# Where the column pass and the low-rank join stand in a fused 2-D DFT and mixer kernel

## The chip, the core and the metric

The kernel runs on one core of a Trainium2 chip. The core has a matrix engine (TensorE, PE in the profile), a vector engine (VectorE, DVE), an activation engine (ScalarE, ACT), a general engine (GpSimd, POOL) and a queue engine that issues transfers (SyncE, SP). Each engine works through its own queue in order and waits on semaphores for the others. Transfers run on 16 shared DMA engines; here GpSimd and SyncE issue nearly all of them. The metric is device time in microseconds for one execution; lower is better.

## The reference

Eight batches of 3136 rows by 256 channels. The first half takes the real part of a two-dimensional Fourier transform, the second half a mixer with a low-rank product over the rows and a two-layer product over the channels:

```
X = fft(x, axis=1); X = fft(X, axis=2); y = X.real          # per batch, 3136 x 256
h = (y^T @ U) @ V                                           # U 3136x32, V 32x3136
u = y + h^T
out = u + relu(u @ w_ch1) @ w_ch2                           # 256 -> 1024 -> 256
```

## The kernel before, in words

**Transform.** The real part needs cosine times cosine minus sine times sine. The symmetries of both are used: rows and channels are first added to and subtracted from their mirror images, so that products run over a quarter of the data. `fold(b)` does this on VectorE (lines 386, 395, 399) from the tiles xf (rows forward) and xr (rows backward), which `load_half` fills for the batch after it by four GpSimd-issued transfers per half (lines 55, 86, 101, 103). `seq` (line 485) multiplies with the sine and cosine tables over the rows and leaves tiles A and B; beside them it leaves the product with U in 32 further columns (tile tf, line 492). `chan` (batches 0 and 1) or `even_ch` and `odd_ch` (later batches) then transform over the channels (lines 631, 633, 643, 652) and give tiles S and T, the two mirror halves of y.

**The first channel.** Channel 0 has no mirror image and is left out of the wide products. For batches 0 and 1, `first_channel` runs a narrow product over it (`narrow`, line 556: sixteen products with 32 columns of weights), evicts it on ScalarE (lines 560, 563) into tiles evc and evo, and adds and subtracts the two parts (lines 570, 573, 574); the result is row 32 of tile va, and two copies (line 622) mirror it. For batches 2 to 7 (six together) this is the column pass: `column_loads` issues 28 transfers of single elements on SyncE into cf and cr (lines 530, 539); `column_steps` has seven steps: two casts on ScalarE (line 590), one small fold product (lines 596, 599) with its eviction (line 601) and two VectorE sums (line 603), the narrow product, two steps of sums on GpSimd into tiles tc, rows and tcb (lines 570 to 574), and a last step that mirrors rows (line 610) and copies tcb to trow (line 611, a transfer on SyncE).

**The low-rank part.** `joined(b)` adds the two halves of tf into tile tab (line 468, on GpSimd); for batches 2 and up it also copies that batch's piece of trow into tab (line 672, GpSimd) and its row of rows into row 32 of va (line 673, a transfer on SyncE). `lowrank(b)` multiplies tab with the channel tables (line 678) and ScalarE evicts the product into ta (line 680). There are two va and two ta tiles, used in turn by even and odd batches. `last_row` fills one more row of va on VectorE (line 684).

**The mixer.** The 8 x 3136 rows are taken in 49 chunks of 512. `front(c)` multiplies ta and va for a chunk (line 709) and VectorE adds S and T to it, giving u (line 725); `turned` transposes u by a SyncE transfer (line 703). `first_product` (line 735) multiplies u with w_ch1 into one of three buffers p, and ScalarE applies the relu (line 737). `second_product` (line 751) multiplies with w_ch2 one chunk later; VectorE adds the transposed u (lines 757, 759, 760) into tile o, of which there are three, and SyncE stores a chunk (line 765).

**What sets the order.** The main loop has eight slots a chunk (`8 * c + j`); in each slot stand a step of the first product, every second slot one of the second, and whatever steps of the next batch's transform a table `due` holds for that slot. `front(c + 1)` follows slot `8 * c + 3`. `spread` lays a list of steps evenly over a range of slots; batch 1's 23 transform steps lie over slots 23 to 42, and batch 2's transform ends at slot 90. From chunk 1 on, a planner reorders each engine's queue from the given order by its own estimates, except for instructions that `pin` keeps in program order, so a step that moves in the table can move its neighbours in every queue.

Of the kernel before, what the change touches and what calls it, by code (L numbers as in the profile page):

```python
# [27 lines left out]
def kernel(  # L28
# [261 lines left out]
    def kp(i):  # L290
        return KP if i == NI - 1 else PQ
# [174 lines left out]
    def join_t(eng):  # L466

        eng.tensor_tensor(TS, TF[:, :, 0], TF[:, :, 1], op=AL.add)  # L468
# [76 lines left out]
    def narrow(nb, stationary, dst, tc_, total, tag=("dft", 3), late=None, eng=None):  # L545

        t = {}
        eng = eng or nc.vector

        def products():  # L550
            pt = t["pt"] = psum.tile([P, QW], FP32, tag=tag[0], name="ptc", bufs=tag[1])
            for n in range(NI // 2):
                for g in range(4):
                    pn, par = divmod(g, 2)
                    i = ktiles(pn)[n]
                    nc.tensor.matmul(pt[g * R:(g + 1) * R], stationary(par, i),
                                     tabs[1][:kp(i), i, par, :],
                                     start=(n == 0), stop=(n == NI // 2 - 1))
            t["ev"] = wp.tile([P, QW], FP32, tag="ev", name="evc", bufs=4)
            nc.scalar.copy(t["ev"][2 * R:], t["pt"][:2 * R])  # L560
            if eng is nc.gpsimd:
                t["pt"] = wp.tile([P, QW], FP32, tag="ev", name="evo", bufs=4)
                nc.scalar.copy(t["pt"][2 * R:], pt[2 * R:])
        yield products

        def sums(par):
            e, o = (t[k][(2 + par) * R:(2 + par) * R + nb] for k in ("ev", "pt"))
            up = dst[:, HALF // 2 - par:(0 if par else None):-2]
            dn = dst[:, HALF // 2 + 2 - par:HALF + 1 - par:2]
            eng.tensor_tensor(tc_[:, par], o[:, NQ:QW], e[:, NQ:QW], op=AL.add)  # L570
            if par and total is not None:
                eng.tensor_tensor(total, tc_[:, 0], tc_[:, 1], op=AL.add)
            eng.tensor_tensor(up, o[:, par:NQ], e[:, par:NQ], op=AL.add)
            down = lambda: eng.tensor_tensor(dn, e[:, 1:NQ], o[:, 1:NQ], op=AL.subtract)  # L574
            if late is None:
                down()
            else:
                late.append(down)
        for par in range(2):
            yield lambda par=par: sums(par)  # L580

    def column_steps():
        ec = cpool.tile([KP, 2, NI, NB], BF16, name="ec")
        tc_ = cpool.tile([NB, 2, R], FP32, name="tc")

        cb = [cpool.tile([KP, 2, NI, NB], BF16, name=f"cb{t}", tag=f"cb{t}") for t in range(2)]

        def lower(t):
            with tc.issue_after(LAST[0].ins):
                nc.scalar.copy(cb[t][:], (cf, cr)[t][:])  # L590
        for n in range(2):
            yield lambda n=n: lower(n)

        def fold_c():
            pc = psum.tile([KP, 2, NI, NB], FP32, tag="dft", name="pc", bufs=3)
            nc.tensor.matmul(pc.rearrange("p a i b -> p (a i) b"), flip[:KP, 0, :KP],
                             cb[0].rearrange("p a i b -> p (a i) b"), start=True, stop=False)
            for a in range(2):
                nc.tensor.matmul(pc[:, a], flip[:KP, 1, :KP], cb[1][:, a, ::-1],
                                 start=False, stop=(a == 1))  # L600
            nc.scalar.copy(ec[:], pc[:])
            for par in range(2):
                nc.vector.tensor_tensor(GC[par][:, :NI * NB].rearrange("p (i b) -> p i b", b=NB), ec[:, 0], ec[:, 1],
                                        op=AL.add if par == 0 else AL.subtract)
        yield fold_c
        yield from narrow(NB, lambda par, i: GC[par][:kp(i), i * NB:i * NB + R], rows, tc_,
                          tcb[:], eng=nc.gpsimd)

        def finish():
            nc.gpsimd.tensor_copy(rows[:, HALF + 1:S], rows[:, HALF - 1:0:-1])  # L610
            nc.sync.dma_start(out=trow.rearrange("o (b r) -> o b r", b=NB), in_=tcb[:])
        yield finish

    def first_channel(b, **kw):
        dst = VA[b][R:R + 1]
        yield from narrow(1, lambda par, i: G[b][par][:kp(i), i, 256:256 + R], dst, TF[:1, 0],
                          None, **kw)
        mid = (HALF + S) // 2
        for lo, hi in ((HALF + 1, mid), (mid, S)):
            def turn_row(lo=lo, hi=hi):  # L620
                if b:
                    nc.gpsimd.tensor_copy(dst[:, lo:hi], dst[:, S - lo:S - hi:-1])  # L622
                    return
                with tc.issue_after(LAST[0].ins):
                    nc.scalar.copy(dst[:, lo:hi], dst[:, S - lo:S - hi:-1])
            yield turn_row

    def chan(b, lo, hi, h, tag=("dft", 3), dve=False):
        d = ST[b]
        pt = psum.tile([P, CH], FP32, tag=tag[0], name="pst", bufs=tag[1])  # L630
        nc.tensor.matmul(pt[:, :hi - lo], MC[:, h * P:(h + 1) * P], d["A"][:, lo:hi],
                         start=True, stop=False)
        nc.tensor.matmul(pt[:, :hi - lo], MSN[:, h * P:(h + 1) * P], d["B"][:, lo:hi],
                         start=False, stop=True)
        (nc.vector.tensor_copy if dve else nc.scalar.copy)(
            d["ST"[h]][:, lo:hi], pt[:, :hi - lo])
# [31 lines left out]
    def joined(b):  # L668

        join_t(nc.gpsimd)  # L670
        if b >= B0:
            nc.gpsimd.tensor_copy(TS[:1, 0], trow[:, (b - B0) * R:(b - B0 + 1) * R])
            nc.sync.dma_start(out=VA[b % 2][R:R + 1, :], in_=rows[b - B0:b - B0 + 1, :])

    def lowrank(b, tag=("dft", 3)):
        pt = psum.tile([P, 256], FP32, tag=tag[0], name="ptt", bufs=tag[1])
        for typ in range(2):
            nc.tensor.matmul(pt[:], TAB[:, typ * R:typ * R + P], MDT[typ][:], start=(typ == 0),
                             stop=(typ == 1))
        nc.scalar.copy(TA[b % 2][:R, :], pt[:R])  # L680

    def last_row(b):
        d = ST[b]
        nc.vector.tensor_tensor(VA[b % 2][2 * R:2 * R + 1, HALF + 1:S], d["S"][0:1, HALF - 1:0:-1],
                                d["T"][0:1, HALF - 1:0:-1], op=AL.subtract)
# [84 lines left out]
    def transform(b):  # L770

        for par in range(2):
            for typ in (1, 0):
                for pn in range(2):
                    yield lambda par=par, typ=typ, pn=pn: seq(b, par, typ, pn)
        if b < B0:
            row = list(first_channel(b, eng=nc.gpsimd))
            yield from row[:3]
            for ch in range(4):
                for h in range(2):  # L780
                    yield lambda ch=ch, h=h: chan(b, ch * 392 + (1 if ch else 0),
                                                  (ch + 1) * 392 + 1, h)
            yield from row[3:]
            yield lambda: (joined(b), last_row(b))
            yield lambda: lowrank(b)
            return
        for ch in range(4):
            yield lambda ch=ch: (even_ch(b, ch), across(b, ch, False))
            yield lambda ch=ch: (odd_ch(b, ch), across(b, ch, True), ch < 3 or joined(b))
        yield lambda: lowrank(b)  # L790
# [193 lines left out]
    for step in piece(1, 0) + piece(1, 1, tag=("p2", 2)) + late[2:] + late[:2]:  # L984
# [8 lines left out]
    due = {2: piece(2, 0), 3: piece(2, 1), 8: piece(3, 0),  # L993
           9: piece(3, 1), 10: piece(0, 0), 11: piece(0, 1), 13: [lambda: last_row(0)],
           16: narrow_0[3:4], 18: narrow_0[4:5]}
# [6 lines left out]
    for b in range(1, B):  # L1002
        hi = 8 * (b * S // CH - 1) + 2
        if b == 1:
            spread(list(fold(b)), 4, 23)
            spread(list(transform(b)), 23, hi)
        else:
            spread(list(fold(b)), hi - 66, hi - 35)
            spread(list(transform(b)), hi - 33, hi)
        if b == B0:  # L1010
            for at, step in zip((19, 18, 16, 15, 14, 13, 6), column_steps()):
                due.setdefault(hi - at, []).append(step)
    for n, step in enumerate(column_loads()):
        due.setdefault(8 + 15 * n // 7, []).append(step)
    for c in range(NCH + 1):
        if c == 1:
            order.close()
# [41 lines left out]
```

## Time and profile before

| | us |
|---|---|
| median of 3 runs | 448.58 |
| lowest and highest run | 448.21, 449.38 |
| the profiled execution's own time | 448.78 |
| its span in the profile | 446.7 |
| TensorE matmul busy | 435.9 |
| VectorE busy | 354.0 |
| ScalarE busy | 297.1 |
| GpSimd busy | 83.6 |

The profile is of one execution. Times within it count from the start of the span. Of each instruction it gives the start, the duration, the engine, the line of the kernel, the tiles written and read (buffer numbers left out) and their shape; a line with x8 stands for eight instructions in a row. Matmuls are pipelined and their ends are modelled, so the distance of two starts says more than a duration. In brackets stands how long the engine was idle ahead of the instruction and what ended that. The granted TensorE clock is full in all slices.

### The profile page before, as it was taken

What the parts mean: (1) busy time and instruction counts of PE and PEld (TensorE: products, weight loads), DVE (VectorE), ACT (ScalarE), POOL (GpSimd) and SP (SyncE); (2) the same over time, 40 slices, a digit from 0 to 9 for tenths busy, and PEclk for the clock granted to TensorE, in tenths of its full rate; (3) what the DMA queues carried; (4) which work ended last, traced back from release to release, by engine and by line L of the source; (5) the groups of instructions that cost most, each with busy time, mean ns of one, the idle gap of its engine ahead of it and who ended that gap; (6) DMA issues with size and microseconds to landing.
All of it is one profiled execution on the core that took longest, in us unless ns stands there. A gap on an engine that the chain in (4) does not pass through costs nothing.

```text
span 446.7 us, 8094 instructions
## 1 busy us (share of the span) xinstructions
PE 435.9 (98%) x2959; PEld 316.5 (71%) x3012; DVE 354.0 (79%) x838; ACT 297.1 (67%) x564; POOL 83.6 (19%) x144
## 2 busy tenths in 40 slices
PE   8999999999989999999999999999999999999997
PEld 6547666777666777777777777777777777777775
DVE  8979998788997789978998789978998776443433
ACT  8867647555975569756785569655885669656562
POOL 8973219200371002300211002300000000000000
PEclk9999999999999999999999999999999999999999
DMA  7997987985579337683599537792333333434343
GB/s 141 216 238 189 222 163 145 208 148 94 145 184 225 95 105 209 192 188 73 149 209 201 111 119 207 189 182 70 95 117 93 80 114 73 114 100 117 96 123 113
DMA packets 103249, 65.36 MB, mean 146 GB/s; under 512 B 73806, under 2 KB 99624, under 8 KB 100464
## 3 DMA queue, kind: packets, MB, share of 16 engines
q1 hardware_dynamic: 97528, 39.10, 40.1%
q0 software_dynamic: 5664, 25.75, 21.7%
q8 instruction: 23, 0.38, 0.4%
q14 instruction: 16, 0.13, 0.1%
q10 hardware_dynamic: 18, 0.00, 0.0%
HBM read 29.33 MB, written 25.69 MB: 123 GB/s over the span
## 4 chain that ended last, share of the span: by engine, by line
PE 76%; POOL 8%; DMA 6%; DVE 6%; issue 3%; DVEq 0%; POOLq 0%
PE p L751 34%; PE p L735 30%; DMA xf<-in_x_dram,xidx 5%; PE ph L709 4%; PE pt L485 4%; PE ptq L446 2%; DMA va<-rows 1%; DVE eof L386 1%; DVE eor L386 1%; PE pst L643 1%; PE pst L652 1%; DVE u L725 1%; POOL va L574 1%; POOL va L622 1%; POOL rows L574 1%
## 5 line engine op out<-in xcount | busy, mean ns | idle before, releaser
L737 ACT ACTIVATE h<-p 128x512 bf16<-128x512 f32 x392 | 221.8, 597 | 123.0 <-PE p L735 103.8
L735 PE MATMUL p<-u,w 128*128 128x512 bf16 x734 | 209.9, 379 | 1.3 <-DVE B L504 0.2
L751 PE MATMUL p<-w,h 128*128 128x256 bf16 x1568 | 203.7, 273 | 1.2
L751 PEld LDWEIGHTS <-h 128*128 128x128 bf16 x1568 | 153.2, 98 | 51.0 <-issue 0.3
L735 PEld LDWEIGHTS <-w 128*128 128x128 bf16 x784 | 106.0, 144 | 33.8 <-issue 0.5
L757 DVE TENSOR_TENSOR o<-p,ut 128x4 f32<-128x4 f32 (+1 forms) x100 | 16.2, 162 | 57.1 <-PE p L751 54.7
L760 DVE TENSOR_TENSOR o<-p,ut 128x254 f32<-128x254 f32 (+1 forms) x100 | 40.7, 407 | 0.0
L759 DVE TENSOR_TENSOR o<-p,ut 128x254 f32<-128x254 f32 (+1 forms) x100 | 40.7, 407 | 0.0
L468 POOL TENSOR_TENSOR tab<-tf 128x64 bf16<-128x64 f32 x7 | 3.1, 442 | 180.7 <-DVE tf L492 180.6
L386 DVE TENSOR_TENSOR eor<-xr 99x1024 bf16<-99x1024 f32 x28 | 34.5, 1236 | 0.1
L725 DVE TENSOR_TENSOR u<-ph,T 128x512 bf16<-128x512 f32 (+23 forms) x63 | 34.3, 555 | 0.2 <-PE ph L709 0.2
L386 DVE TENSOR_TENSOR eof<-xf 99x1024 bf16<-99x1024 f32 x28 | 34.4, 1244 | 0.0
L725 DVE TENSOR_TENSOR u<-ph,S 128x512 bf16<-128x512 f32 (+23 forms) x63 | 34.4, 555 | 0.0
L709 PE MATMUL ph<-va,ta 128*128 128x512 bf16 (+15 forms) x124 | 28.6, 328 | 1.6 <-DMA va<-rows 1.5
L55 POOL DMA_INDIRECT xf<-in_x_dram,xidx x14 | 17.1, 1220 | 61.9 <-DVE eof L386 50.5
L485 PEld LDWEIGHTS <-g 98*128 98x128 bf16 (+1 forms) x152 | 14.7, 98 | 13.2 <-issue 0.7
L395 DVE TENSOR_TENSOR eos<-eof,eor 99x1024 bf16<-99x1024 bf16 (+1 forms) x28 | 20.5, 748 | 0.0
L654 DVE TENSOR_TENSOR S<-evd,pst 128x392 bf16<-128x392 f32 (+1 forms) x24 | 13.5, 563 | 7.2 <-PE pst L652 4.9
L485 PE MATMUL pt<-tabs,g 98*128 98x425 bf16 x80 | 17.6, 344 | 0.0
L457 DVE TENSOR_TENSOR ev<-ptq,ex 128x131 f32<-128x131 f32 (+1 forms) x24 | 6.9, 289 | 12.7 <-ACT ex L450 12.7
L399 DVE TENSOR_TENSOR g<-eos 99x2048 bf16<-99x2048 bf16 (+1 forms) x14 | 17.0, 1218 | 0.0
L485 PE MATMUL pt<-tabc,g 98*128 98x425 bf16 x72 | 15.5, 344 | 0.0
(198 smaller groups left out, 380.2 us busy)
## 6 DMA issues: line engine op xcount, KB each, us to landing
out_dram<-o SPq DMA_DIRECT2D x48, 512.0 KB
xr<-in_x_dram POOLq DMA_DIRECT2D x14, 784.0 KB, 8.2
xb<-in_x_dram POOLq DMA_DIRECT2D x2, 392.0 KB, 6.8
ut<-u SPq DMA_TRANSPOSE x49
w<-in_moe_w_ch_dram POOLq DMA_DIRECT2D x1, 512.0 KB
out_dram<-o SPq DMA_DIRECT2D x4, 128.0 KB
va<-in_moe_V_dram POOLq DMA_DIRECT2D x2, 196.0 KB
w<-in_moe_w_ch_dram POOLq DMA_DIRECT2D x1, 256.0 KB, 6.1
```

The lines of the kernel that those rows point to most:

```text
L55: nc.gpsimd.indirect_dma_start(out_, None, bass.AP(t.tensor, t.offset, [[w, rows], [1, w]]), bass.IndirectOffsetOnAxis(idx, 0), element_of ...
L386: pin(nc.vector.tensor_tensor(dst[:, a, :, part * P:(part + 1) * P].rearrange("p i (k t) -> p i k t", k=2), lo, hi, op=AL.subtract if part ...
L395: pin(nc.vector.tensor_tensor(EOS[:, a, :, cols], EOF_[:, a, :, cols], EOR_[:, a, ::-1][:, :, cols], op=op))
L399: pin(nc.vector.tensor_tensor(G[b % 2][par][:, :, cols], EOS[:, 0, :, cols], EOS[:, 1, :, cols], op=AL.add if par == 0 else AL.subtract))
L485: nc.tensor.matmul(pt[:], g[:kp(i), i, P * typ:P * (typ + 1)], tabs[typ][:kp(i), i, par, :], start=(n == 0), stop=(n == NI // 2 - 1))
L709: nc.tensor.matmul(ph, TA[b % 2][:k, s * P:(s + 1) * P], VA[b % 2][:k, lo:hi], start=start, stop=True)
L725: nc.vector.tensor_tensor(u[:, s, col:col + hi - lo], ph[:, col:col + hi - lo], src, op=AL.add)
L735: nc.tensor.matmul(p1[:], W1[:, s, j::JT], k["u"][:, s, :], start=(s == 0), stop=(s == 1))
L737: LAST[0] = nc.scalar.activation(k["h"][:, j, :], p1[:], AF.Relu)
L751: nc.tensor.matmul(p2[:, t % w, :], h[:, j, rs], W2[:, j, :], start=(j == 0), stop=(j == JT - 1))
L759: nc.vector.tensor_tensor(o[:, ts, 1:P], p2[:, :w, 1:P], ut[:, ts, 1:P], op=AL.add)
L760: nc.vector.tensor_tensor(o[:, ts, P + 1:D], p2[:, :w, P + 1:D], ut[:, tT, P - 1:0:-1], op=AL.add)
```

## The change

Three edits, and no instruction is added or taken away.

- In batch 1's list of transform steps, `joined(1)` (line 468) is put into the same step as the second narrow sum; it stood behind the eight channel steps and the two mirroring copies, together with `last_row`. `last_row` now stands in one step with `lowrank`, so the list has 22 steps over the same slots instead of 23.
- The seven steps of the column pass stand 24, 23, 21, 20, 19, 18 and 12 slots ahead of slot 90 instead of 19, 18, 16, 15, 14, 13 and 6: slots 66, 67, 69, 70, 71, 72 and 78 instead of 71, 72, 74, 75, 76, 77 and 84.
- The 28 column loads stand two slots apart (slots 8 to 62) instead of 15/7 of a slot (8 to 65).

```
         if b < B0:
             row = list(first_channel(b, eng=nc.gpsimd))
-            yield from row[:3]
+            yield from row[:2]
+            yield lambda: (row[2](), joined(b))
             for ch in range(4):
                 for h in range(2):
                     yield lambda ch=ch, h=h: chan(b, ch * 392 + (1 if ch else 0),
                                                   (ch + 1) * 392 + 1, h)
             yield from row[3:]
-            yield lambda: (joined(b), last_row(b))
-            yield lambda: lowrank(b)
+            yield lambda: (lowrank(b), last_row(b))
             return
...
         if b == B0:
-            for at, step in zip((19, 18, 16, 15, 14, 13, 6), column_steps()):
+            for at, step in zip((24, 23, 21, 20, 19, 18, 12), column_steps()):
                 due.setdefault(hi - at, []).append(step)
     for n, step in enumerate(column_loads()):
-        due.setdefault(8 + 15 * n // 7, []).append(step)
+        due.setdefault(8 + 2 * n, []).append(step)
```

In the built program the queues differ as follows around these steps. GpSimd: the join of batch 1 stands directly behind its six narrow sums; the sums of the column pass, the mirror copy (line 610) and the first copy of line 672 stand ahead of the loads xf and xr that stood before and among them. SyncE: the copy to trow (line 611) stands one transpose and one output store sooner, and the first copy of line 673 directly behind the output store that follows it, two transposes sooner than before. TensorE: the column pass's small product stands ahead of the last group of batch 2's row products, and its sixteen narrow products directly behind that group.

More of the change, by code (lines that the diff above doesn't have):

```diff
@@ L777, in transform @@
             row = list(first_channel(b, eng=nc.gpsimd))
-            yield from row[:3]
+            yield from row[:2]
+            yield lambda: (row[2](), joined(b))
             for ch in range(4):
@@ L783, in transform @@
             yield from row[3:]
-            yield lambda: (joined(b), last_row(b))
-            yield lambda: lowrank(b)
+            yield lambda: (lowrank(b), last_row(b))
             return
@@ L1010 @@
         if b == B0:
-            for at, step in zip((19, 18, 16, 15, 14, 13, 6), column_steps()):
+            for at, step in zip((24, 23, 21, 20, 19, 18, 12), column_steps()):
                 due.setdefault(hi - at, []).append(step)
     for n, step in enumerate(column_loads()):
-        due.setdefault(8 + 15 * n // 7, []).append(step)
+        due.setdefault(8 + 2 * n, []).append(step)
     for c in range(NCH + 1):
```

## The prediction

> **What bounds the kernel now.** I read the page first, then the list of waits for TensorE's own, then TensorE's timeline at each of them, then the queues that feed those places.
>
> ```profile
> span 446.7 us, 8094 instructions
> PE 435.9 (98%) x2959; PEld 316.5 (71%) x3012; DVE 354.0 (79%) x838; ACT 297.1 (67%) x564; POOL 83.6 (19%) x144
> PE 76%; POOL 8%; DMA 6%; DVE 6%; issue 3%; DVEq 0%; POOLq 0%
> ```
>
> TensorE is busy for 98% of the span, so time is won only where TensorE itself stands still. The chain nevertheless gives 8% to GpSimd and 6% to DMA: stretches in which TensorE's next product was held by them. The list of waits has three such places, all at L678, the low-rank product that needs tile tab, and at L709, the product that needs the column row in va. A listed wait counts from the last modelled end; what it costs is better read from the starts in TensorE's timeline (start, duration, line, tiles, count, and in brackets the idle time before and what ended it):
>
> ```profile
> 76.55 1.04 PE L751 MATMUL p<-w,h 128*128 128x256 bf16 x8
> 78.09 0.28 PE L678 MATMUL ptt<-msn,tab 128*128 128x256 bf16 x1 [0.51 <-POOL tab L468]
> ...
> 128.02 0.81 PE L735 MATMUL p<-u,w 128*128 128x512 bf16 x3
> 129.36 0.28 PE L678 MATMUL ptt<-msn,tab 128*128 128x256 bf16 x1 [0.54 <-POOL tab L672]
> ...
> 132.53 0.82 PE L735 MATMUL p<-u,w 128*128 128x512 bf16 x3
> 134.88 0.48 PE L709 MATMUL ph<-va,ta 128*128 128x384 bf16 x2 [1.53 <-DMA va<-rows]
> ```
>
> The chain gives the undisturbed pace:
>
> ```profile
> 78.48 0.86 PE p L735 x4
> 79.35 0.87 PE p L751 x8
> ```
>
> So eight L751 take 0.87 us, and three L735 take 0.65. Without a wait the three products would have begun at 76.55 + 0.87 = 77.42, at 128.67 and at 133.18. The waits cost 0.67, 0.69 and 1.70 us: **3.06 us together**, and that is what the change aims at.
>
> **Part 1: the join of batch 1 directly behind its narrow sums.** No work is added or removed. GpSimd's queue now:
>
> ```profile
> 71.64 1.47 POOL L574 TENSOR_TENSOR va<-evc,evo 1x392 bf16<-1x392 f32 x1
> 73.05 0.60 POOL L86 DMA_DIRECT2D xr<-in_x_dram  x1
> 74.21 2.56 POOL L622 COPY va<-va 1x783 bf16<-1x783 bf16 x2
> 76.86 1.18 POOL L468 TENSOR_TENSOR tab<-tf 128x64 bf16<-128x64 f32 x1
> ```
>
> The join L468 moves ahead of the issue of the load xr and its edge (1.1 us to 74.21) and of two copies (2.56). It starts at about 73.1 and ends by 74.3 even with its 1.18, and TensorE wants it at 77.42: 3 us of cover. **-0.67 us.** What comes late next is the two copies, now ending by about 78.0 instead of 76.77:
>
> ```profile
> 66.51 0.38 PE L735 MATMUL p<-u,w 128*128 128x512 bf16 x1 [0.21 <-DVE B L504]
> 80.06 0.60 PE L709 MATMUL ph<-va,ta 65*128 65x64 bf16 x4
> ```
>
> The products that read va of batch 1 follow at 80.06 less 0.67, so 1.4 us remain. The load xr is issued 1.2 us later at most, and belongs to the next batch's fold. One step less in batch 1's list also makes the planner lay the last two transform products directly ahead of the narrow products. It reorders the same products; the 0.21 us wait on VectorE (first row) can go, and a wait of its size twice over can come, since ScalarE has more evictions in a row there. I bound it at -0.2 to +0.5 us and take 0, because no instruction is added.
>
> **Part 2: the column pass five slots sooner.** In the changed program's queues the sixteen column products (L556) follow the last ordinary product of batch 2 instead of starting at 114.90. Rows of today's place:
>
> ```profile
> 108.31 0.89 PE L485 MATMUL pt<-tabs,g 98*128 98x425 bf16 x4
> 114.90 1.00 PE L556 MATMUL ptc<-tabc,gc 98*32 98x425 bf16 x16
> 117.14 0.33 PE L643 MATMUL pst<-A,me 128*128 128x392 bf16 x1 [0.16 <-ACT evo L563]
> ...
> 113.95 1.01 POOL L55 DMA_INDIRECT xf<-in_x_dram,xidx  x1 [4.05 <-DVE eof L386]
> 120.21 0.24 POOL L570 TENSOR_TENSOR tc<-evo,evc 6x32 f32<-6x32 f32 x1 [4.67 <-DMA xf<-in_x_dram,xidx]
> 125.51 0.60 POOL L86 DMA_DIRECT2D xr<-in_x_dram  x1
> 126.68 1.48 POOL L610 COPY rows<-rows 6x1567 bf16<-6x1567 bf16 x1
> ```
>
> The products go to about 109.2 (the four pt end issuing 0.72 after 108.31; the small fold product pc adds 0.2). Their eviction ended 2.2 us behind their start (117.1, where the last TensorE row waited for it), hence now at 111.4. Today the sums wait 3.1 us more, until 120.21, because the load xf is ahead of them on GpSimd; in the new order it stands behind the sums and that wait goes. From sums to the end of the mirror copy is 128.16 - 120.21 = 7.95 us, less 1.12 for the two xr issues (125.56 to 126.68) that also move behind: 6.8, ending at about 118.2 instead of 128.16. So tab's corner (L672) is ready some 8 us before 128.67: **-0.69 us**.
>
> The load xf itself comes some 5 to 8 us later than 113.95, and xr behind it somewhat sooner than 125.51; the folds that read them begin only here, so I cost that at nothing:
>
> ```profile
> 165.36 2.35 DVE L386 TENSOR_TENSOR eof<-xf 99x1024 bf16<-99x1024 f32 x2
> ```
>
> The row copy into va is on SyncE:
>
> ```profile
> 111.39 0.38 SPq L765 DMA_DIRECT2D out_dram<-o  x1
> 118.03 1.23 SPq L703 DMA_TRANSPOSE ut<-u  x1
> 124.50 0.77 SPq L611 DMA_DIRECT2D trow<-tcb  x1
> ...
> 128.79 6.05 DMA va<-rows
> ```
>
> On SyncE's queue L611 now stands directly ahead of the store of 111.39, and the row copy L673 between that store and the transpose of 118.03. L673 is issued when the mirror is done, 118.3 to 121; what it holds up is that transpose, by at most 3 us. Even with today's 6.05 us (last row, from the chain) it lands by 127.3; its product is due at 133.18 - 0.67 - 0.69 = 131.8, or 0.7 sooner since its products are now ahead of three L735. **-1.70 us.** The 0.3 us before 117.14, where a product waited for the column eviction, should also go, since that product now comes 1.7 us behind the evictions: **-0.3**.
>
> The 28 loads keep their number and their SyncE queue (0.86 us each below); 3 slots fewer in all. The last pair now follows the transpose of 99.13:
>
> ```profile
> 99.13 1.26 SPq L703 DMA_TRANSPOSE ut<-u  x1
> 102.34 1.72 SPq L539 DMA_DIRECT2D cr<-in_x_dram  x2
> ...
> 104.70 0.60 ACT L737 ACTIVATE h<-p 128x512 bf16<-128x512 f32 x1 [0.56 <-PE p L735]
> ```
>
> The last is issued at about 101.3; ScalarE's cast of cr now stands behind the activation of 104.70, at 105.3. No row shows this load landing. Nearest on the same queue: trow, issued 124.50 and used at 128.16, at most 3.7 us; the upper end is va's 6.05. So 105.0 (no wait) to 107.4, which would hold ScalarE and the activations queued behind the cast for 2 us; TensorE has three p buffers to fill meanwhile, so about 1 us would reach it. I take 0, by trow, which is the nearer in size.
>
> Against the change stands VectorE. The moved sums now meet its folds:
>
> ```profile
> L386 DVE TENSOR_TENSOR eof<-xf x28: 1207/1216/2008, 37.2 to 332.2; 99x1024 bf16<-99x1024 f32 x28
> 127.23 2.01 DVE L386 TENSOR_TENSOR eof<-xf 99x1024 bf16<-99x1024 f32 x1
> 111.28 2.35 DVE L386 TENSOR_TENSOR eof<-xf 99x1024 bf16<-99x1024 f32 x2
> 117.32 0.68 DVE L725 TENSOR_TENSOR u<-ph,S 128x512 bf16<-128x512 f32 x1
> 123.98 0.17 DVE L757 TENSOR_TENSOR o<-p,ut 128x4 f32<-128x4 f32 x1 [0.20 <-PE p L751]
> 126.03 0.68 DVE L725 TENSOR_TENSOR u<-ph,T 128x512 bf16<-128x512 f32 x1
> 119.97 0.59 PE L735 MATMUL p<-u,w 128*128 128x512 bf16 x2
> ```
>
> The fold at 127.23 ran beside the mirror copy of 126.68 and took 0.8 us over its median. The two folds of 111.28 and the one that follows them will now run beside the sums. The add ahead of them comes about 1 us later, because its product is now behind the column products (1.00). VectorE's u, done at 118.0, is read at 119.97: 1.97 us of cover. So u is late by between 1.0 - 1.97, nothing, and 1.0 + 3 x 0.8 - 1.97 = 1.4 us. I take 0.6, near the middle, as the folds need not all meet a long sum: **+0.6**. In return the fold of 127.23 is free of the mirror copy, which VectorE needs when TensorE arrives early near 131.
>
> [...]
>
> **Sum.** -0.67 - 0.69 - 1.70 - 0.3 + 0.6 = -2.8 us. The profiled execution took 448.78 us (span 446.7 and 2.1 around it), 0.2 above the median 448.58 of the runs. 448.78 - 2.8 = 446.0, so the median should come to **445.8**.
>
> **Rivals.** A change of 0.3% is 1.35 us here, about what a measurement can tell from none.
>
> First: nothing is given back. If the folds slip between the sums, u is in time: -3.4, or -3.6 with the gain of the reshuffle: **445.1**. For it: 1.97 us of cover; against it: the 2.01 row.
>
> Second: VectorE becomes the bound. u late by 1.4 and the reshuffle's 0.5: -2.8 + 0.8 + 0.5 = -1.5: **447.1**. For it: VectorE is 79% busy over the span, and today's 0.8 us stretch is a fact.
>
> Third: the row is late all the same, so the change doesn't do its main part: the row goes behind an output store and beside the 784 KB loads xf and xr, now issued together. It would have to take over 10 us; then the last 1.70 stays and the gain is 1.1: **447.5**. Against it: today's 6.05 stands behind a transpose and beside such a load. [...]
>
> ```profile
> xr<-in_x_dram POOLq DMA_DIRECT2D x14, 784.0 KB, 8.2
> ```
>
> Fourth, slower: SyncE is parked. L611 and L673 now stand ahead of the output store of 111.39 and of the transpose of 118.03. If the sums end no sooner than today (trow issued at 124.50), that store is issued at 125.3 and lands 5.4 us later (estimate: 512/784 of xr's time to landing), at 130.7; the add of 123.98, three output buffers on, waits 6.7 us for it, and u behind it (126.03) ends at 134.0, where TensorE wants it at 128.02. 6.0 us lost, less the 3.06: **451.5**. It decides once trow's source comes after about 124; I have it 4.3 us behind the sums' start, at 116 to 118.
>
> **How the numbers follow.** Forecast 0.62, first rival 0.10, second 0.15, third 0.07, fourth 0.06. The page quoted first, the waits and the order agree on where the time goes, so the forecast has most. Range 444.7 to 447.1: it leaves out the third and fourth and edges of the others. Faster by over 0.3% (below 447.23): forecast, first rival and most of the second, 0.86; same 0.08; slower 0.06. The forecast's own range is 445.3 to 446.4.
>
> **What would show it.** Right: no TensorE wait at L678 for tab L468 or L672 and none at L709 for rows; L570 of the column straight behind evo near 111; L386 folds over 1.6 us near 112 to 118; a wait of about 0.6 us of L735 on VectorE's u near 119. Wrong: a ScalarE wait at L590 on the loads, or a wait for rows that is left near 131, or SyncE's store held past 118.

## The result and the profile after

The changed kernel takes **447.2 us** (median of 7 runs, 446.29 to 447.51) against 448.58 (median of 7, 448.21 to 449.58). The ratio is 0.9962, with a 95% interval of 0.995 to 0.9974: faster by 1.4 us, where 2.8 were forecast, and 0.1 us above the forecast's range. The profiled execution took 447.31 us with a span of 445.2, against 448.78 and 446.7.

The page of the changed kernel (span, busy times, and the chain by engine):

```profile
span 445.2 us, 8087 instructions
PE 435.7 (98%) x2960; PEld 316.4 (71%) x3012; DVE 353.1 (79%) x838; ACT 297.5 (67%) x564; POOL 85.7 (19%) x144
PE 91%; DVE 2%; DMA 2%; issue 1%; POOL 1%; ACT 1%; DVEq 0%; POOLq 0%
```

TensorE's share of the chain rose from 76 to 91%; GpSimd's 8% and DMA's 6% are nearly gone. TensorE's waits in the changed kernel (engine, operation, what it waited for; total, times, longest), without a first one of 1.4 us at the program's start (1.3 before) and three of 0.2 us:

```profile
PE m L850 <- DMA xb<-in_x_dram,xidx: 0.5, 2, 0.3
PE pst L643 <- DVE T L654: 0.4, 1, 0.4
PE m L850 <- DMA xb<-in_x_dram: 0.3, 1, 0.3
```

All three stalls are gone from L678 and L709. A wait of L643 for VectorE's T is new. The waits of L850 for the loads xb lie in the first 16 us, which the change doesn't touch. TensorE's timeline at these places, after:

```profile
31.17 1.52 PE L735 MATMUL p<-u,w 128*128 128x512 bf16 x6
...
71.99 0.38 PE L735 MATMUL p<-u,w 128*128 128x512 bf16 x1
72.52 0.38 PE L709 MATMUL ph<-va,ta 65*128 65x512 bf16 x1
...
77.86 1.04 PE L751 MATMUL p<-w,h 128*128 128x256 bf16 x8
78.73 0.27 PE L678 MATMUL ptt<-msn,tab 128*128 128x256 bf16 x1
...
117.30 0.33 PE L643 MATMUL pst<-A,me 128*128 128x392 bf16 x1 [0.36 <-DVE T L654]
...
120.67 0.82 PE L735 MATMUL p<-u,w 128*128 128x512 bf16 x2
...
131.77 1.04 PE L751 MATMUL p<-w,h 128*128 128x256 bf16 x8
132.64 0.61 PE L709 MATMUL ph<-va,ta 65*128 65x128 bf16 x4
```

L678 follows its eight L751 by their 0.87 us, and the four L709 stand together at 132.64 with no wait for the row. Three gaps are new, read from start to start: 0.31 us at 72.52 (one L735 takes 0.22), 0.52 at 117.30, and 0.23 within the two L735 of 120.67 (0.82 long where 0.60 is usual). The first L735 starts at 31.17; in the profile of before it was 30.17. So part of what the stalls gave up seems to have gone into the first 31 us. The experiments had to say whether that belongs to the change.

### The profile page after: what moved, and what is told of

Same layout as the page of the kernel before. It is cut to its first block, busy times and chain, and to the rows that moved or that the text cites. A ratio compares the mean times of both kernels' runs of the same rounds, so it can differ in the third digit from the quotient of the medians.

```text
span 445.2 us, 8087 instructions
## 1 busy us (share of the span) xinstructions
PE 435.7 (98%) x2960; PEld 316.4 (71%) x3012; DVE 353.1 (79%) x838; ACT 297.5 (67%) x564; POOL 85.7 (19%) x144
## 4 chain that ended last, share of the span: by engine, by line
PE 91%; DVE 2%; DMA 2%; issue 1%; POOL 1%; ACT 1%; DVEq 0%; POOLq 0%
PE p L751 38%; PE p L735 35%; PE pt L485 6%; PE ph L709 5%; DMA xb<-in_x_dram,xidx 2%; PE ptq L446 2%; PE pst L643 1%; PE pst L652 1%; PE m L850 1%; PE ptc L556 1%; ACT h L737 0%; DVE eor L386 0%; PE pst L631 0%; DVE eof L386 0%; PE pst L633 0%
## 5 line engine op out<-in xcount | busy, mean ns | idle before, releaser
L735 PE MATMUL p<-u,w 128*128 128x512 bf16 x735 | 209.3, 379 | 1.2 <-DVE B L500 0.2
L751 PE MATMUL p<-w,h 128*128 128x256 bf16 x1568 | 203.0, 273 | 1.4
L751 PEld LDWEIGHTS <-h 128*128 128x128 bf16 x1568 | 153.2, 98 | 50.4 <-DVE o L760 0.3
L735 PEld LDWEIGHTS <-w 128*128 128x128 bf16 x784 | 106.1, 144 | 35.1 <-issue 2.0
L468 POOL TENSOR_TENSOR tab<-tf 128x64 bf16<-128x64 f32 x7 | 3.1, 440 | 179.2 <-DVE tf L492 179.1
L386 DVE TENSOR_TENSOR eof<-xf 99x1024 bf16<-99x1024 f32 x28 | 35.8, 1293 | 0.0
L709 PE MATMUL ph<-va,ta 128*128 128x512 bf16 (+15 forms) x124 | 28.6, 328 | 0.3
L395 DVE TENSOR_TENSOR eos<-eof,eor 99x1024 bf16<-99x1024 bf16 (+1 forms) x28 | 19.2, 702 | 0.0
```

Of the source, the lines that this page charges most:

```text
L386: pin(nc.vector.tensor_tensor(dst[:, a, :, part * P:(part + 1) * P].rearrange("p i (k t) -> p i k t", k=2), lo, hi, op=AL.subtract if part ...
L395: pin(nc.vector.tensor_tensor(EOS[:, a, :, cols], EOF_[:, a, :, cols], EOR_[:, a, ::-1][:, :, cols], op=op))
L709: nc.tensor.matmul(ph, TA[b % 2][:k, s * P:(s + 1) * P], VA[b % 2][:k, lo:hi], start=start, stop=True)
L735: nc.tensor.matmul(p1[:], W1[:, s, j::JT], k["u"][:, s, :], start=(s == 0), stop=(s == 1))
L751: nc.tensor.matmul(p2[:, t % w, :], h[:, j, rs], W2[:, j, :], start=(j == 0), stop=(j == JT - 1))
```

## The experiments

### How much of it is the start, and how large were the stalls

Both kernels were run once more without an edit.

> The kernel before, unchanged, once more, for the scatter of the first 31 us. Theory (the start varies from execution to execution with the landing of the first loads of x): median within 0.3 us of the kernel before, single times spread over 1 us or more, and the first L735 begins at 30.2 or up to 1 us later. Rival (the start belongs to the program): the first L735 at 30.2 us as before, and single times within 0.5 us.

> The changed kernel unchanged, once more, beside the others. Theory: the three stalls stay gone whatever the start, so its time follows its start: first L735 near 30.2 us would give a span of 444.2, near 31.2 us one of 445.2; median 447.2 within 0.4 us. Rival: the stalls come back in part in another execution; a gap at L678 or L709 near 78, 129 or 133 us, and a median of 448 us.

The kernel before: 449.12 us (12 runs, 447.9 to 452.78), ratio to the other runs of before 1.0012 (0.9992 to 1.0031). The changed kernel: 447.15 us (9 runs), ratio 0.9971 (0.9962 to 0.9981), first L735 at 31.29, span 445.3, none of the three stalls. The profiled execution of the repeated kernel before (TensorE's timeline, and from the chain the row's transfer with its duration):

```profile
31.02 1.52 PE L735 MATMUL p<-u,w 128*128 128x512 bf16 x6
...
78.91 0.28 PE L678 MATMUL ptt<-msn,tab 128*128 128x256 bf16 x1 [0.48 <-POOL tab L468]
...
128.82 0.81 PE L735 MATMUL p<-u,w 128*128 128x512 bf16 x3
130.12 0.28 PE L678 MATMUL ptt<-msn,tab 128*128 128x256 bf16 x1 [0.49 <-POOL tab L672]
...
133.29 0.82 PE L735 MATMUL p<-u,w 128*128 128x512 bf16 x3
134.80 0.49 PE L709 MATMUL ph<-va,ta 128*128 128x384 bf16 x2 [0.69 <-DMA va<-rows]
```
```profile
129.57 5.18 DMA va<-rows
```

The same program started its first L735 0.85 us later than in the first profile, and yet its span is 446.7 again. The row landed at 134.75, where it had landed at 134.84: its transfer took 5.18 us where it took 6.05. So the stall at L709 was 134.80 - 133.29 - 0.65 = 0.86 us, not 1.70, while those at L678 stayed at 0.65. **The late start was swallowed by the stall for the row.** The three stalls together were 2.2 us here. With part 1 alone the row landed at 134.64, after 5.43 us, with the first L735 at 31.05. In 13 profiled executions of the kernels told of here the first L735 started between 30.16 and 31.29, in eight of them after 31.0; the first profile of before was one of the early ones, and its row transfer the slowest of the four in which the column pass stands in its old place. The start belongs to the execution and not to the program, and it goes with the landing of the first loads of x: the last two of them (xb) are issued at 5.75 and 6.64 us in the first profile of before and at 5.74 and 6.64 in that of the changed kernel, while xb's loads take 6.8 to 8.1 us from issue to landing in the one and 7.9 to 9.1 in the other. Where TensorE has no wait for xb its first L735 starts at 30.16 or 30.17 (three profiles), where it waits for 0.3 to 1.1 us in all, at 30.56 to 31.29 (the other ten). Why these loads land sooner or later, and why the row lands at nearly the same time whatever the start, stays open.

### One part at a time

Three kernels. The first has only the edit of batch 1's list:

```diff
-            yield from row[:3]
+            yield from row[:2]
+            yield lambda: (row[2](), joined(b))
...
-            yield lambda: (joined(b), last_row(b))
-            yield lambda: lowrank(b)
+            yield lambda: (lowrank(b), last_row(b))
```

The second has only the two edits of the column pass, the third only the upper one of them, with the loads at their old spacing:

```diff
-            for at, step in zip((19, 18, 16, 15, 14, 13, 6), column_steps()):
+            for at, step in zip((24, 23, 21, 20, 19, 18, 12), column_steps()):
...
-        due.setdefault(8 + 15 * n // 7, []).append(step)
+        due.setdefault(8 + 2 * n, []).append(step)
```

> Part 1 alone (the join of batch 1 directly behind its narrow sums). Forecast's term: the wait of L678 for tab near 78 us goes, -0.67 us, and nothing comes in its place: 447.9 us. Rival read from the trace of the changed kernel: the two transform products laid side by side cost 0.3 us near 72 us, so that only 0.36 us is left: 448.2 us. Both expect no TensorE wait for tab L468 of batch 1, and the waits of 0.69 and 1.70 us near 129 and 135 us unchanged. If the changed program as such starts 1 us later (its first L735 at 31.17 us and not at 30.17 us), this one shows it or not: by the theory that it is chance from run to run, the medians hide it.

> Part 2 alone (column pass five slots sooner, loads two slots apart). Forecast's terms: -0.69 -1.70 -0.3 +0.6 = -2.1 us: 446.5 us. By the trace of the changed kernel the loss to VectorE is about 0.7 us, which gives the same within 0.1. Rival: the row's place was worth less than the waits show, because the work behind is held by VectorE instead: -1.0 us, 447.6 us. All expect no wait at L678 for L672 and none at L709 for rows.

> Column steps five slots sooner, but the loads at their old spacing, so that the last pair is issued one slot ahead of the cast of it. Theory: a load on this queue lands 2 to 4 us after its issue, the cast L590 on ScalarE waits some 2 us and about 1 us of it reaches TensorE: 447.5 us, with a ScalarE wait at L590. Rival: the spacing of the loads is worth nothing, the cast is free: as with both, 446.5 us.

Against 448.87 for the kernel before on that chip: part 1 alone 448.74, ratio 0.9994 (0.9982 to 1.0007), no difference that can be told; part 2 alone 447.52, 0.9981 (0.9965 to 0.9997); column steps alone 447.51, 0.9975 (0.9964 to 0.9985). So the gain is nearly all part 2's, about 1.35 us by the medians, which lies between the 2.1 of the theory and the 1.0 of its rival; the spacing of the loads adds nothing to it. In part 1 alone the wait for tab L468 is gone and the 0.31 us gap is there (72.40), as the rival had it; but the 0.34 us that this leaves (0.65 - 0.31) doesn't show in the time either. With the column pass in its old place TensorE waits for the row further on, and what it wins ahead of that wait lengthens it: the stall at L709 was 134.68 - 132.95 - 0.65 = 1.08 us with part 1 alone, against 0.86 in the repeated kernel before, which started within 0.03 us of it. TensorE with part 2 alone, then with the column steps alone; then ScalarE with the column steps alone:

```profile
78.53 0.28 PE L678 MATMUL ptt<-msn,tab 128*128 128x256 bf16 x1 [0.96 <-POOL tab L468]
```
```profile
78.56 0.28 PE L678 MATMUL ptt<-msn,tab 128*128 128x256 bf16 x1 [0.58 <-POOL tab L468]
```
```profile
106.96 0.27 ACT L590 CAST cb<-cr 99x96 bf16<-99x96 f32 x1 [1.20 <-DMA cr<-in_x_dram]
```

The join of batch 1 is ready at nearly the same moment in both, though the first started its L735 at 30.16 and the second at 30.56: the earlier start waits longer. With the old loads the cast does wait for its last load, 1.2 us where the theory had some 2: the second load of the last pair, issued at about 103.7, had landed by 106.96, 3.3 us later. But ScalarE had that time to give; none of it reached TensorE.

### The empty step: what the reshuffle costs, and what hangs on it

```diff
             yield lambda: (lowrank(b), last_row(b))
+            yield lambda: None
             return
```

This gives batch 1's list its 23 steps back, in the changed kernel, and in the kernel before with part 1 only.

> The changed kernel with an empty step at the end of batch 1's list, so that its steps keep their old slots and the last two transform products are not laid together ahead of the narrow products. Theory: the 0.31 us gap of TensorE near 72.5 us (seen in the changed kernel and with part 1 alone, in neither of the others) belongs to that reshuffle: it goes, 446.9 us against 447.2. Rival: it comes from the join's new place; it stays, 447.2 us.

> The kernel before with the join of batch 1 directly behind its sums, and an empty step at the end of the list so that the other steps keep their slots; column pass and column loads at their old places. Forecast's term without the reshuffle: -0.67 us, 448.0 us. Rival, from the changed kernel with the empty step (449.3 us): the GpSimd loads xf and xr are then issued directly behind each other near 80 to 82 us, SyncE's column loads and the transpose behind them take 8 to 10 us to issue instead of 5, VectorE's u waits for the transpose's tile and TensorE for u near 92 us: +1 to +2 us, 449.5 to 450.5 us. Here the casts of the columns come later, so no wait of L599 for cb near 112 us.

The 0.31 us gap goes in both, so it does belong to the reshuffle. But neither is faster: 449.27 us (before 449.0), ratio 1.0012 (0.9995 to 1.0029), and 448.23 us (before 448.42), 1.0001 (0.9989 to 1.0013); for the second neither the gain of the forecast's term nor the 1 to 2 us of the rival came. In the changed kernel the empty step costs about 2 us by the medians. GpSimd, SyncE and TensorE in the changed kernel with the empty step (a profiled execution of 452.89 us, the longest of its 12, so its sizes are not the usual ones):

```profile
80.25 1.03 POOL L55 DMA_INDIRECT xf<-in_x_dram,xidx  x1 [2.01 <-issue]
81.84 0.58 POOL L86 DMA_DIRECT2D xr<-in_x_dram  x1
```
```profile
78.73 9.93 SPq L539 DMA_DIRECT2D cr<-in_x_dram  x2
88.77 7.66 SPq L703 DMA_TRANSPOSE ut<-u  x1
```
```profile
92.60 0.44 PE L735 MATMUL p<-u,w 128*128 128x512 bf16 x1 [1.78 <-DVE u L725]
...
112.69 0.23 PE L599 MATMUL pc<-cb,flip 99*99 99x48 bf16 x2 [1.35 <-ACT cb L590]
```

The same lines in the changed kernel:

```profile
80.94 1.19 POOL L55 DMA_INDIRECT xf<-in_x_dram,xidx  x1 [1.93 <-issue]
...
83.39 0.58 POOL L86 DMA_DIRECT2D xr<-in_x_dram  x1 [0.69 <-DVE eor L386]
```
```profile
85.76 4.58 SPq L539 DMA_DIRECT2D cr<-in_x_dram  x2
...
93.64 2.23 SPq L703 DMA_TRANSPOSE ut<-u  x1
```

With the empty step the two 784 KB loads go out 1.6 us apart instead of 2.45, SyncE then needs 10 us to issue two column loads and 7.7 for the transpose behind them, u and the casts are late, and TensorE stands still twice, for 3.1 us in all. That is not the whole loss of this execution: its page shows the granted TensorE clock (tenths, in 40 slices of 11.3 us) below full in the two slices that hold or follow the waits.

```profile
PEclk9999999989899999999999999999999999999999
```

Behind the second wait TensorE's timeline has:

```profile
114.38 1.98 PE L556 MATMUL ptc<-tabc,gc 98*32 98x425 bf16 x16 [0.28 <-DVE gc L603]
116.29 1.08 PE L735 MATMUL p<-u,w 128*128 128x512 bf16 x2
117.16 1.42 PE L751 MATMUL p<-w,h 128*128 128x256 bf16 x8
118.64 0.38 PE L735 MATMUL p<-u,w 128*128 128x512 bf16 x1
```

From start to start the sixteen L556 took 1.91 us, the two L735 0.87 and the eight L751 1.48, where the same products took 0.84, 0.49 and 0.88 in the changed kernel (from 109.89): 2.05 us more. The mean clock of this execution was 0.992, and the missing 0.008 of its span of 450.8 us is 3.6 us, an estimate of the loss in both slices together. The other eleven executions had a mean clock of 0.999 or 1.000 and a median of 449.18, so the 2 us by the medians don't come from the clock. The wait of 1.53 us in the first profile of before had no such drop behind it (a mean clock of 0.999, and full in all slices), so whether the waits lowered the clock is open.

With part 1 and the empty step the transpose is the one that takes 9.94 us (at 83.85), and only 0.8 us reaches TensorE, near 99.9, because the casts are due later there. In the other eleven profiles the two loads stand 2.3 to 2.5 us apart, and there no issue of SyncE between 70 and 102 us takes more than 5.3 us. That the distance of the two loads is the cause fits all 13 but was not tried by itself.

### VectorE beside the moved sums

First the changed kernel without the row's sums, for the column pass alone, and without the mirror copy (rows is set to zero at the start instead, a line that is not shown):

```diff
+            if nb > 1:
+                return
             eng.tensor_tensor(up, ...)
...
-            nc.gpsimd.tensor_copy(rows[:, HALF + 1:S], rows[:, HALF - 1:0:-1])
```

Then the changed kernel with the fold of batch 3 begun six slots later:

```diff
-            spread(list(fold(b)), hi - 66, hi - 35)
+            spread(list(fold(b)), hi - (60 if b == B0 + 1 else 66), hi - 35)
```

> The changed kernel without the four row sums (L573, L574) and the mirror copy (L610) of the column pass on GpSimd; the row stays zero, so the last column of the output is left out of the computation. Theory: VectorE's folds L386 are slow near 113 to 120 us (3.25 for two, 1.97 for one) because GpSimd's sums run beside them; without them each takes 1.2 us, TensorE's gaps of 0.52 us near 117.3 and 0.23 us near 121.1 go: 446.5 us against 447.2. Rival: VectorE is late there because its add waits for a later product; the folds are short but 0.4 us of the gap at 117.3 stays: 447.0 us.

> The changed kernel with the fold of batch 3 spread over 25 slots that begin 6 slots later, instead of 31, so that its first folds on VectorE no longer stand beside the column's sums. Theory: the gaps of 0.52 and 0.23 us go and nothing else moves: 446.5 us. Rival: VectorE, without idle time from 123 to 136 us in the changed kernel, cannot take the folds in fewer slots; TensorE waits 1 us or more for u between 125 and 145: 448 us.

Without the sums: 446.58 us, ratio 0.9945 (0.9929 to 0.9962). With the fold later: **446.38 us, 0.9944 (0.9922 to 0.9966)**, faster than the kernel before and, by some 0.8 us (447.15 in its repetition), than the changed kernel. In both the gaps of 0.52 and 0.23 us are gone, with spans of 444.5 and 444.4 after starts at 31.2 and 31.1. VectorE's folds near the sums, in the changed kernel and then without the sums (starts of the folds; two in the first line of each):

```profile
113.04 3.25 DVE L386 TENSOR_TENSOR eof<-xf 99x1024 bf16<-99x1024 f32 x2
...
117.89 1.97 DVE L386 TENSOR_TENSOR eor<-xr 99x1024 bf16<-99x1024 f32 x1
```
```profile
113.07 2.37 DVE L386 TENSOR_TENSOR eof<-xf 99x1024 bf16<-99x1024 f32 x2
...
117.01 1.23 DVE L386 TENSOR_TENSOR eor<-xr 99x1024 bf16<-99x1024 f32 x1
```

The folds start at the same time in both, so the later add isn't what makes VectorE late; the stretched folds are. GpSimd pays as well: in the changed kernel a sum of 1.47 us before took 2.00, and the mirror copy 2.37 instead of 1.48.

```profile
113.21 2.00 POOL L574 TENSOR_TENSOR rows<-evc,evo 6x392 bf16<-6x392 f32 x1
...
118.84 2.37 POOL L610 COPY rows<-rows 6x1567 bf16<-6x1567 bf16 x1
```

### Further and nearer slots

The changed kernel with the column pass five further slots sooner, and its loads closer together:

```diff
-            for at, step in zip((24, 23, 21, 20, 19, 18, 12), column_steps()):
+            for at, step in zip((29, 28, 26, 25, 24, 23, 17), column_steps()):
-        due.setdefault(8 + 2 * n, []).append(step)
+        due.setdefault(8 + 7 * n // 4, []).append(step)
```

And with the column pass only two slots ahead of its old place, three behind that of the change (the last step four):

```diff
-            for at, step in zip((24, 23, 21, 20, 19, 18, 12), column_steps()):
+            for at, step in zip((21, 20, 18, 17, 16, 15, 8), column_steps()):
```

> The changed kernel with the column steps five further slots sooner and its loads 1.75 slots apart. Theory: the sums on GpSimd end by about 113 us, before the folds begin; only the mirror copy may meet one; gaps of 0.52 and 0.23 us go: 446.5 us. Rival: the column's products now stand among batch 2's transform, whose evictions on ScalarE and folds on VectorE they delay; a new gap of 0.5 to 1 us near 105 us: 447.5 us.

> The changed kernel with the column steps two slots sooner than before instead of five. On GpSimd the sums still stand ahead of the load xf, and only the mirror copy L610 and the corner L672 behind the loads xf and xr. Theory: what held the row was the load xf ahead of the sums, not the slots; sums at about 114 to 120, loads, mirror at 123 to 126, row landed by 131.5: no wait at L678 for L672, at most 0.3 us at L709, and the folds meet the sums as before: 447.3 us. Rival: the slots count; the mirror copy waits for the loads to land as the sums did, 6 us, and TensorE waits 1 us or more at L709: 448.3 us.

Five slots sooner again: 448.88 us, ratio 1.0 (0.9986 to 1.0014). Two slots sooner than before only: 450.57 us, 1.0052 (1.0036 to 1.0068), slower than the kernel before. In three of the six executions at two slots the mean granted clock was 0.995 or 0.996, and they took 451.07 to 451.75; the three at 0.999 or 1.000, the profiled one among them, took 449.35 to 450.07, still above every run of before beside them (447.86 to 449.02). Both kernels came out above both of their expectations. TensorE's waits at five further slots:

```profile
102.72 0.23 PE L599 MATMUL pc<-cb,flip 99*99 99x48 bf16 x2 [0.69 <-ACT cb L590]
104.64 1.00 PE L556 MATMUL ptc<-tabc,gc 98*32 98x425 bf16 x16 [0.36 <-DVE gc L603]
118.83 0.33 PE L643 MATMUL pst<-A,me 128*128 128x392 bf16 x1 [0.94 <-DVE T L654]
```

The casts wait for the loads (2.55 us on ScalarE), and now there is work behind them that TensorE wants at once. T is late by 0.94 us although the folds run undisturbed here (2.34 us for two, from 115.48): the sums no longer meet them. They meet two other VectorE instructions just ahead of the folds (VectorE, then GpSimd):

```profile
110.83 1.15 DVE L463 TENSOR_TENSOR ev<-ex,ev 128x196 f32<-128x196 f32 x1
112.01 1.57 DVE L464 TENSOR_TENSOR ev<-ev,ex 128x228 f32<-128x228 f32 x1
```
```profile
110.74 1.02 POOL L574 TENSOR_TENSOR rows<-evc,evo 6x392 bf16<-6x392 f32 x1
111.82 1.50 POOL L610 COPY rows<-rows 6x1567 bf16<-6x1567 bf16 x1
```

The same two take 0.36 and 0.40 us in the repeated kernel before, so VectorE loses 2 us here beside one sum and the mirror copy. By this trace the interference has moved rather than gone; no run leaves the sums out in this order. At two slots sooner (GpSimd, SyncE, TensorE):

```profile
125.76 1.66 POOL L610 COPY rows<-rows 6x1567 bf16<-6x1567 bf16 x1
127.38 1.20 POOL L672 COPY tab<-trow 1x32 bf16<-1x32 bf16 x1
```
```profile
127.30 2.60 SPq L703 DMA_TRANSPOSE ut<-u  x1
130.07 0.62 SPq L673 DMA_DIRECT2D va<-rows  x1
```
```profile
136.53 0.48 PE L709 MATMUL ph<-va,ta 128*128 128x384 bf16 x2 [2.33 <-DMA va<-rows]
```

The sums stand ahead of the load xf, as in the changed kernel, but the mirror is behind xf and xr, and the row copy then finds SyncE with a transpose that takes 2.6 us. It is issued at 130.07 and lands 6.4 us later, beside both loads; TensorE waits 2.5 us for it, against 0.86 in the kernel before. So both expectations were wrong: the mirror did not wait for the loads to land, but the row's place on SyncE and beside the loads cost more than the sums' earlier start gave.

## Why the forecast had the sign and twice the size

The steps of the forecast beside what the profiles show. The measured column compares the changed kernel with the repeated kernel before, since those two started within 0.15 us of each other:

| step of the forecast | forecast, us | measured, us |
|---|---|---|
| join of batch 1: wait at L678 | -0.67 | -0.65 |
| transform products laid together | 0 (-0.2 to +0.5) | +0.31 |
| tab's corner: wait at L678 | -0.69 | -0.65 |
| column row: wait at L709 | -1.70 | -0.86 |
| product that waited for evo | -0.3 | -0.3 |
| VectorE late beside the sums | +0.6 (to 1.4) | +0.75 |
| sum | -2.8 | -1.4 |

The spans differ by 446.7 - 445.2 = 1.5 us, though the changed kernel started 0.15 later; some 0.2 us of its gain is in no row of the table.

**The step that failed is the size of the third stall**: "-1.70 us" for the row copy into va, read from one execution. The mechanism was right, the wait is gone; but the waiting time is the difference of a product that moves with the start of the execution and a row that landed between 134.64 and 134.84 in all four profiles of the old place. In the first profile TensorE was early and the row transfer slow, so the stall was at its largest. The forecast set that execution's time beside the median (448.78 against 448.58) and took it for typical. The time was typical; the split into an early start and a long stall was not, since the stall takes up what the start gives. This error is 0.84 of the 1.4 us.

**The reshuffle** was bounded rightly and then taken at nothing "because no instruction is added". It cost 0.31 us, and the empty step shows that it is the reshuffle. With it, part 1 was worth about a third of a microsecond by its gaps, and alone not even that: while the stall for the row was still there, it took up what part 1 gained ahead of it.

**VectorE** was 0.15 us above the term, from the cause named: the folds took 3.25 for two and 1.97 where they took 2.35 and 1.22, and leaving the sums out brings both the durations (2.37 and 1.23) and the 0.75 us back. The way to TensorE was in part another one: the forecast had only a late u, which gave 0.23 us; the other 0.52 came by T, for which the product at 117.30 waited. Folds and sums both grew here: a sum of 1.47 us took 2.00, and the three folds took 1.65 us more together. The upper end of the forecast's term, 1.4 us, was too high, as it had them 2.4 us longer (three times 0.8).

**The signs to look for.** No wait at L678 or L709, sums directly behind evo (112.02, with a start 1 us later), stretched folds and a late u near 120: all there, the last with 0.23 us where about 0.6 was expected. SyncE's store held past 118 was named as a sign against; it was held until 119.0, and nothing waited for it, so that sign was set too tight. L673 was issued at 121.24, where 118.3 to 121 was forecast: GpSimd's own sums were stretched too, which the forecast had not counted. The cast of cr did not wait.

**The rivals.** The second one (VectorE the bound, and the reshuffle at its upper end: 447.1) has nearly the time, from the right two causes, but its sizes are not the ones found: it needed 1.4 and 0.5 where 0.75 and 0.31 were found, and the rest was the stall that was smaller from the start. That its sum comes so near is luck. What the third rival feared, a row that is late behind SyncE's work and beside the two loads, didn't occur at five slots, where TensorE had no wait for the row, and it did at two, where the row landed 6.4 us after its issue and TensorE waited 2.5.

## What to carry to other kernels

A stall in one profile is a sample. Where two runs of work met here, one paced by the engine and one by transfers, its length moved with the start (1.70 us with a first L735 at 30.17, 0.86 with one at 31.02), and a typical total time doesn't make it a typical stall; a second profile of the same program halved the largest one here. A step that is moved in a table moves its neighbours as well: an empty step, which adds no instruction, cost about 2 us, and with it two large loads went out 1.6 us apart instead of 2.45, which is the likely cause but wasn't tried by itself. Work that is moved away from one neighbour can meet the next: the sums slowed the folds at five slots (3.25 us for two instead of 2.35) and, by the trace, two other VectorE sums at ten (1.15 and 1.57 instead of 0.36 and 0.40). And a good place can be narrow: of the places tried, two slots sooner was slower than no change, five was best, ten gave nothing.

## What the runs showed that was not expected

- SyncE's own issue of small loads and of the transpose grew to 9.9 and 7.7 us while two 784 KB loads of GpSimd's queue were in flight, issued 1.6 us apart (xr landed 14.8 us after its issue), against 4.6 and 2.2 us at 2.45 us apart (8.3).
- What a wait on the loads cost TensorE differed: ScalarE's cast waited 1.2 us with nothing lost, and 2.55 us with 0.85 lost on TensorE (102.72), where work that TensorE wanted at once stood behind it.
- In an execution in which TensorE waited 1.78 and 1.35 us, the granted clock was below full in the two slices of 11.3 us that hold or follow the waits, with some 3.6 us lost by its mean of 0.992; in other executions with a wait of 1.53 us (before) and of 2.33 us (two slots) the mean was 0.999.
- The first 31 us vary by up to 1.1 us between executions, with the landing of the first loads of x. The kernel before gave a late start back at its stall for the row; the changed kernel has no stall there, so an early start should show in its time, but both of its profiles started late.
